# A windowed-attention and feed-forward kernel with a written-out plan: split first transposes, later masks and sink values, a new load order

## The chip, the cores and the metric

The kernel runs on one core of a Trainium2 chip. The metric is device time in microseconds (us) of one execution. Its engines are PE (matrix multiply), DVE (vector), ACT (scalar, exponentials), POOL (here it issues the loads from memory and a few small fills) and SP (here it issues stores and DMA transposes).

## The reference

```python
scores = scale * np.matmul(q, k.transpose(0, 1, 3, 2))      # (4, 8, 768, 64) inputs
keep = is_sink | in_window                                  # 4 sink keys, window of 128 back
a = softmax(np.where(keep, scores, -1e9))
attn = np.matmul(a, v)                                      # 4 batches x 8 heads
x = attn.transpose(0, 2, 1, 3).reshape(3072, 512)
out = ((x @ w1) * (x @ w2)) @ w3 @ w_out                    # (3072, 512) fp32
```

Attention over a sliding window with four sink keys feeds a two-branch product network. w1 and w2 are 512 x 1024, w3 is 1024 x 1024, w_out 1024 x 512.

## The kernel before

**The work.** The kernel folds w3 and w_out into one matrix `w3o` of 1024 x 512 at the start, so each token block needs gates (line 744: x times w1 and x times w2), a product (759) and one projection (774). Attention and network are done per batch b = 0..3, in two halves c of 384 tokens. Heads go in pairs r = 0..3. In a half, q and k are transposed (`qkT`), scores (588) go to the PSUM ring `sc`, ACT makes exponentials (606), DVE multiplies by a mask (612), PE multiplies by v and by the sink values (664, ring `av` of one bank), DVE normalises (674, 679) into `xs`, and `xs` is transposed into `xT` for the gates. Matmul results that are not scores or av go through the three banks of the ring `mm`.

**The fold.** The first KA = 3 row blocks of w3 are transposed for each of eight columns j (350), copied (`w3t`, five buffers) and accumulated for all j (358); the accumulation holds one `sc` pair and one `mm` bank from its first group to its last. Row blocks 3 to 7 follow singly (381 transposes, 388 products). Each needs `w3-i`, and the products need all of w_out (`wo-0-1` to `wo-6-8`).

**q and k.** Batch 0 loads blocks of heads (`early`) and transposes them on PE (438). Its first two head pairs come by separate fp32 loads on SP and ACT and are cast (234). Batch 1 loads blocks of 128 tokens (`near`) and transposes them on PE (461). Batches 2 and 3 load into `big`, which the fold must have left, and are transposed by DMA on SP (478), as are their `xs` (720). A name such as `q1-5` in the list of loads is tensor, batch and block.

**The order.** Every step is an `Op` with an engine (or either of ACT and DVE), a guessed duration, dependencies, a priority (a smaller number goes first) and ring buffers that it takes and frees. A planner written in the kernel simulates the engines when the program is built: at each step it takes the operation that can start with the least wait, then the one of the best priority. Its choice is the order of the instructions on each engine, and nothing is reordered on the chip. POOL is the exception: it takes its operations in the order of the list `LOADS`, at most eight loads in flight. A load's guessed landing is the running total of transfer times plus `LAND`, plus a margin `unsure`; a DMA transpose or store issued before 120 us gets a margin `LATE`. These margins change no instruction, only when the planner counts on data. Where it sees a gap on PE before 45 us it fills it with multiplications of zeros (853).

Priorities: the fold's steps have FOLD_J + j and FOLD_I + 4i; batch 0's attention 1 to 4; later attention `1000 + 200 * (b - 1) + LEAD + 200 * SPREAD * part`, where `part` goes from 0 to 1 through a batch; gates of batch b `1000 + 200 * b + 100 * c + 8 * dt`; projections from `1150 + 200 * b + 100 * c`. A load of batch 3 waits for transposes of batch 2, and for the landing of the batch 3 load DEEP places back.

The masks for batches 1 to 3 are made by `late_masks` (261, 263), the sink values of a batch by `sv` (512).

Of the kernel before, what the change touches and what calls it, by code (L numbers as in the profile page):

```python
# [21 lines left out]
def kernel(  # L22
# [22 lines left out]
    P = 128  # L45
# [3 lines left out]
    QC = NB // NC  # L49
    TOK = QC * P  # L50
# [16 lines left out]
    ident = home("ident", [P, P])  # L67
    tri = home("tri", [P, P])
    maskt = home("maskt", [P, 1, 12 * P])
    vst = home("vst", [P, B, D], FP32)  # L70
    pick = home("pick", [P, H], FP32)
# [10 lines left out]
    qN = {0: early[0], 1: near[0]}  # L82
    kN = {0: early[1], 1: near[1]}
# [24 lines left out]
    class Ring:  # L108
# [9 lines left out]
        a=a_home, ab=ab_home, o=o_home, sc=sc_home, av=av_home, mm=mm_home).items()}  # L118
# [1 line left out]
    HOP = 0.12  # L120
    LAND = 1.9
    TUS = 1.3
    LATE = 2.0
    ops = []

    class Op:
# [11 lines left out]
    PE, ACT, DVE, POOL, SP = "pe", "act", "dve", "pool", "sp"  # L138
    EITHER = (ACT, DVE)
    turn_of = [None]  # L140

    def copy(out, in_):
        (nc.scalar.copy if turn_of[0] == ACT else nc.vector.tensor_copy)(out, in_)  # L143

    def cols(n, k=1):
        return k * (n / 2400.0 + 0.0025)

    def act_us(n):
        return 0.165 + n / 1200.0

    def dve_us(n, x=1.0):
        return 0.15 + n / 960.0 / x
# [12 lines left out]
    def pool_op(us, fn, deps=()):  # L165
        return Op(POOL, us, fn, deps)

    KA, LEAD, SPREAD = 3, -30, 0.9
    FOLD_J, FOLD_I = 3.5, 1010
    DEEP = 3  # L170
    FUSED = (1, 2, 3)
    KINDS = (0, 2, 2, 2)
    QK_BY_DMA = ((2, 0), (2, 1), (3, 0), (3, 1))
    X_BY_DMA = ((2, 0), (2, 1), (3, 0), (3, 1))

# [46 lines left out]
    op_vst = []  # L222
# [8 lines left out]
    got = {}  # L231
# [5 lines left out]
    for r in range(2):  # L237
        for n, dst in enumerate((kN, qN)):
            i = 2 * r + n
            got["kq"[n], 0, 0, r] = cast((DVE, ACT)[n], 0.5, dst[0][:, 0, 2 * r:2 * r + 2, :],  # L240
                                         first_home[i][:, 0:TOK].rearrange("p (h m) -> p h m", h=2), st[i])
    LOADS = """k0-0-4 v0-0 ident q0-0-4 pick w3j-2-4 v0-1 tri v0-2 w3j-0-1 w3j-4-6 w3j-1-2 wo-0-1 w3-6
        wo-1-2 wo-2-4 w3j-6-8 wo-4-6 wo-6-8 w3-5 w3-3 w3-4 v0-5 w3-7 k1-4 q0-1-0 k0-1-0 w2 w0 w3
        v0-3 k1-0 v0-4 w1 q1-0 q1-1 k1-1 q1-2 k2-1 q1-3 v1-2 k1-2 k1-5 k2-2 v1-1 v1-0 q1-4 q2-1
        q2-2 k2-0 k1-3 v2-0 q1-5 q2-0 v1-3 q3-5 v1-4 q3-0 v3-2 k2-3 q2-3 k2-5 v3-0 v1-5 k2-4 v2-2
        q2-4 q3-2 q2-5 v3-5 k3-0 v2-1 k3-5 k3-4 q3-3 v2-5 v3-4 k3-2 k3-1 v2-4 q3-1 v3-1 v3-3 k3-3
        q3-4 v2-3"""

    def masks(part):
        m = maskt[:, 0, :].rearrange("p (k q) -> p k q", q=P)  # L250
# [27 lines left out]
    for key in LOADS.split():  # L278
        n = [int(x) for x in key[2 if key[:2] == "wo" else 3 if key[:3] == "w3j" else 1:].split("-") if x.isdigit()]
        if key == "ident":  # L280
            op_ident = pool_op(0.3, lambda: nc.gpsimd.affine_select(
                ident[:], ident[:], compare_op=ALU.is_equal, fill=0.0, base=0, pattern=[[1, P]],
                channel_multiplier=-1), [op_i1])
# [21 lines left out]
        elif key[0] in "kq":  # L305
            _, c, h0 = n
# [8 lines left out]
    op_mask_late = Op(DVE, 0.7, late_masks, [op_mask], prio=30)  # L315
    op_cols = Op(DVE, 0.35, pick_cols, [op_pick], prio=3)
# [11 lines left out]
    fold_done = []  # L328
# [15 lines left out]
    for j in range(KFF):  # L344
        x = []
# [14 lines left out]
        a = Op(PE, cols(P, KA), t3, [got["w3j", j], op_ident], FOLD_J + j, takes=["mm"])  # L360
# [14 lines left out]
    for i in range(KA, KFF):  # L375
        x, y = [], []
# [16 lines left out]
        pr = FOLD_I + 4 * i  # L393
        a = Op(PE, cols(P, KFF), t3, [got["w3", i], op_ident], pr, takes=["mm"])
# [4 lines left out]
        fold_done.append(m_)  # L399
        fold_done.append(Op(EITHER, (act_us(DM), dve_us(DM)), fmc, [m_], 0, frees=[(m0, "mm")]))  # L400

    for late in in_big:
        late.deps += fold_done
    pieces = {
# [12 lines left out]
    for b in range(B):  # L417
        kind = KINDS[b]
        T = qkT_home[b % 2]
# [3 lines left out]
        tp_of = {}  # L423
        base = 10 * b

        def when(part, early):
            return 1000 + 200 * (b - 1) + LEAD + 200 * SPREAD * part if b else early
        if b == 0:
            for c in range(NC):
                for r in range(NP):  # L430
                    x = []

                    def tps(b=b, c=c, r=r, x=x):
                        tp = transposed(x[0].slot["mm"], 6 * P).rearrange("p (s j m) -> p s j m", s=2, m=P)
                        for s, src in ((0, kN[b]), (1, qN[b])):
                            for j in range(QC):
                                for e in range(2):
                                    nc.tensor.transpose(tp[64 * e:64 * e + 64, s, j, :],  # L438
                                                        src[:, c, 2 * r + e, j * D:(j + 1) * D], ident[:])

                    def tpc(T=T, c=c, r=r, x=x):
                        tp = transposed(x[0].slot["mm"], 6 * P).rearrange("p (s j m) -> p s j m", s=2, m=P)
                        for s in range(2):
                            copy(
                                T[:, r, s, c * TOK:(c + 1) * TOK].rearrange("p (m j) -> p m j", j=QC),
                                tp[:, s, :, :].rearrange("p j m -> p m j"))
                    a = Op(PE, cols(P, 6) + 0.12, tps, [got["k", b, c, r], got["q", b, c, r], op_ident],
                           base + 1 + r * 0.1, takes=["mm"])
                    x.append(a)
                    tp_of[c, r] = Op(EITHER, (2 * act_us(3 * P), 2 * dve_us(3 * P)), tpc, [a],  # L450
                                     base + 1, frees=[(a, "mm")])
        else:
            for c in range(NC):
                for r in range(NP) if (b, c) not in QK_BY_DMA else ():
                    x = []

                    def tps(b=b, c=c, r=r, x=x):
                        tp = transposed(x[0].slot["mm"], 6 * P).rearrange("p (s j m) -> p s j m", s=2, m=P)
                        for s, src in ((0, kN[b]), (1, qN[b])):
                            for j in range(QC):  # L460
                                nc.tensor.transpose(tp[:, s, j, :],
                                                    src[:, QC * c + j, r * P:(r + 1) * P], ident[:])

                    def tpc(T=T, c=c, r=r, x=x):
                        copy(
                            T[:, r, :, c * TOK:(c + 1) * TOK],
                            transposed(x[0].slot["mm"], 6 * P).rearrange("p (s m) -> p s m", s=2))
                    a = Op(PE, cols(P, 6), tps,
                           [got[n, b, QC * c + j] for n in "kq" for j in range(QC)] + [op_ident] + war,
                           when((r / 4 + c) / 2 - 0.1 if kind != 1 else r / 4 + c / 50 - 0.1, 0), takes=["mm"])  # L470
                    x.append(a)
                    tp_of[c, r] = Op(EITHER, (act_us(6 * P), dve_us(6 * P, 2)), tpc, [a], base + 1, frees=[(a, "mm")])
        turned = {}
        if any((b, c) in QK_BY_DMA for c in range(NC)):
            for kb in range(NB):
# [21 lines left out]

        def tdep(c, r, b=b, tp_of=tp_of, turned=turned):
            return sum(([turned[s, kb] for s in range(2) for kb in range(3 * c_, 3 * c_ + 3)]
                        if (b, c_) in QK_BY_DMA else [tp_of[c_, r]] for c_ in range(c + 1)), [])  # L500

        def sk(b=b, T=T):
            for e in range(2):
# [5 lines left out]
        x = []  # L509
# [3 lines left out]
                                 vst[:, b:b + 1, :].to_broadcast([P, H, D]),  # L513
                                 pick[:, :, None].to_broadcast([P, H, D]))
        warv = list(all_av[b - 2]) if b >= 2 else []
        op_sv = Op(DVE, dve_us(512), sv, op_vst + [op_cols] + warv, when(0, base + 2))

        groups = [(2, 3), (3, 6)] if kind != 1 else [(2, 6)]
        op_es, sinks_at = {}, {}
        for q0, q1 in groups:  # L520
            x = []
# [12 lines left out]
            if b in FUSED:  # L534
                at = (1 if q0 == 2 else 5 if kind == 0 else 3)
# [3 lines left out]
            a = Op(PE, cols(w) + 0.22, ss, [op_sk] + sum([tdep(c, r) for c in cs for r in range(NP)], []) + warv,  # L539
                   when(0.5 if q0 == 3 else 0, base + 2), takes=["mm"])  # L540
# [24 lines left out]
        for n_v, visit in enumerate(visits):  # L565
            x = []
# [60 lines left out]
        for n_u, (c, r) in enumerate(order):  # L627
            x = []
# [13 lines left out]
            frees = []  # L642
# [23 lines left out]
            a = Op(PE, us, avf, list(dict.fromkeys(deps)), when(n_u / 8, base + 3 + 0.01 * n_u), takes=["av"] + (["xs"] if first else []), frees=frees)  # L666
# [21 lines left out]
        for c in range(NC):  # L688
            holder = [None]
            if (b, c) not in X_BY_DMA:  # L690
                evs = []
                for n_h in range(2):
                    x = [holder]
# [9 lines left out]
                    def xtc(n_h=n_h, x=x):  # L703
                        copy(x[0][0].slot["xT"][:, 2 * n_h:2 * n_h + 2, :],
                                              transposed(x[1].slot["mm"], 6 * P).rearrange("p (r m) -> p r m", r=2))
                    a = Op(PE, cols(P, 6), xtp, [norm[c, 2 * n_h], norm[c, 2 * n_h + 1]], when(c / 2 + (n_h + 1) / 4 if kind != 1 else n_h / 2 + 0.5, base + 2.5), takes=["mm"],
                           frees=[(xs_first[c], "xs")] if n_h else [])
                    x.append(a)
                    ev = Op(EITHER, (act_us(6 * P), dve_us(6 * P, 2)), xtc, [a] + ([holder[0]] if n_h else []), base + 2.5,
                            takes=["xT"] if n_h == 0 else [], frees=[(a, "mm")])  # L710
# [5 lines left out]
            else:  # L716
                evs = []
                for j in range(QC):
                    def xtd(c=c, j=j, holder=holder, xs_first=xs_first):
# [3 lines left out]
                            takes=["xT"] if j == 0 else [],  # L723
                            frees=[(xs_first[c], "xs")] if j == QC - 1 else [])
# [7 lines left out]
    for b in range(B):  # L732
        for c in range(NC):
# [3 lines left out]
            for dt in range(KFF):  # L737
                pr = 1000 + 200 * b + 100 * c + 8 * dt
                x = [holder]
# [10 lines left out]
                def acopy(y=y):  # L750
# [4 lines left out]
                        takes=["mm"], frees=[(holder, "xT")] if dt == KFF - 1 else [])  # L755
                y.append(g2)

                def amul(dt=dt, y=y, abh=abh):
                    nc.vector.tensor_mul(abh[0].slot["ab"][:, dt, :], y[1].slot["a"][:], y[2].slot["mm"][:, 0:TOK])  # L759
                am_ = Op(DVE, dve_us(TOK), amul, [g2, ac] + ([abh[0]] if dt else []), 0, takes=["ab"] if dt == 0 else [],  # L760
                         frees=[(g2, "mm"), (ac, "a")])
# [3 lines left out]
            for mi in range(QC):  # L765
                m = QC * c + mi
                x = []
                last, oh = b == B - 1 and m == NB - 1, []
                for n0, n1 in ([(0, 256), (256, 384), (384, 512)] if last else [(0, 512)]):
                    x = []  # L770
# [33 lines left out]
    ready = {e: [o for o in ops if e in o.us_on and not o.missing] for e in free}  # L804

    def unsure(at):
        return 0.0 if at < 40.0 else 1.0

    def wants(o, e):
        at = max([d.done + (0.0 if d.ran == e == PE else HOP) for d in o.deps], default=0.0)  # L810
# [124 lines left out]
```

## Time and profile before

| what | value |
|---|---|
| median of 8 runs | 200.91 us (200.4 to 201.48) |
| the profiled execution: time, span | 200.4 us, 198.7 us |
| busy PE, DVE, ACT, POOL | 191.1, 112.6, 100.2, 73.0 us |
| granted PE clock | 1.00 |
| gates (744), projections (774) | 512 and 208 matmuls, busy 89.9 and 45.6 us |
| DMA queue of the loads | 91.6% of 16 engines' span |

The span runs from the first to the last instruction; the profiled execution's own time has 1.7 us around it. Times in the text are from the start of the span. A row of the timeline gives start, duration, engine, line, operation, destination and sources, count and, in brackets, the idle time of the engine before it and what ended it. A row of the waits gives the waiting instruction, what released it, total wait, times and longest wait. Matmuls overlap: one of 512 columns shows 379 ns, but four in a row end 0.86 us after the first began, 0.216 each.

A load's landing is when its completion count arrives. Landings in the order of issue, for the loads that the text names: w3j-0-1 12.40, wo-0-1 15.17, w3-6 16.44, wo-1-2 17.08, wo-6-8 22.32, q0-1-0 30.97, k0-1-0 33.00, w2 35.63, w0 38.35, w1 46.27, k1-2 53.46, q1-5 68.00, v1-3 70.81.

### The profile page before, as it was taken

The page shows a single profiled execution, that of the slowest core. Times are in us where ns is not written, and L with a number is a line of the kernel's source. Part 1 is how long each engine was busy: PE and PEld are TensorE (multiplying, and loading weights), DVE is VectorE, ACT ScalarE, POOL GpSimd, SP SyncE. Part 2 cuts the span into 40 slices and gives each one's busy share as a digit, 9 for nine tenths or more (in the row PEclk, how much of TensorE's full clock was granted, in tenths as well). Part 3 has the DMA queues.
Part 4 walks back from the last instruction along what each step waited for, and adds up shares of the span by engine and source line. Part 5 has one row for each costly group of instructions (what it writes and reads, how often), then busy time and mean ns, then how long its engine had stood idle before and what let it go on. Part 6 is the DMA issues. An engine that isn't in the chain of part 4 may idle for free.

```text
span 198.7 us, 4523 instructions
## 1 busy us (share of the span) xinstructions
PE 191.1 (96%) x1815; PEld 116.8 (59%) x1815; DVE 112.6 (57%) x258; ACT 100.2 (50%) x162; POOL 73.0 (37%) x96
## 2 busy tenths in 40 slices
PE   7979999999999799999999999999999999999993
PEld 6746555556666565666566556555665566555443
DVE  3987313688579588877388633435886653324200
ACT  3785444864375387663356723348377324343232
POOL 7996673687983676925930000000000000000000
PEclk9999999999999999999999999999999999999999
DMA  6999999999999999999999235554504225020133
GB/s 173 175 174 196 204 186 195 194 176 159 154 171 159 154 157 131 169 120 154 173 201 159 35 127 148 147 105 101 116 0 105 83 79 111 0 106 0 56 124 140
DMA packets 98181, 26.42 MB, mean 133 GB/s; under 512 B 86896, under 2 KB 94576, under 8 KB 98160
## 3 DMA queue, kind: packets, MB, share of 16 engines
q0 software_dynamic: 73584, 14.29, 91.6%
q1 hardware_dynamic: 23888, 11.38, 27.1%
q10 hardware_dynamic: 688, 0.46, 0.7%
q8 instruction: 14, 0.23, 0.5%
q14 instruction: 7, 0.06, 0.1%
HBM read 29.39 MB, written 6.29 MB: 180 GB/s over the span
## 4 chain that ended last, share of the span: by engine, by line
PE 60%; DMA 24%; POOL 9%; SPq 2%; issue 2%; ACT 0%; POOLq 0%
PE mm L744 30%; PE mm L774 19%; DMA w_sb<-in_moe_w_dram 10%; DMA big<-in_moe_w_dram 8%; DMA near<-in_q_dram 6%; PE av L664 5%; PE sc L588 4%; POOL big L160 4%; POOL vN L160 3%; POOL near L160 1%; SPq L478 1%; DMA qkT<-big 1%; POOL early L160 1%; SPq L720 1%; PE mm L700 1%
## 5 line engine op out<-in xcount | busy, mean ns | idle before, releaser
L744 PE MATMUL mm<-xT,w_sb 128*128 128x384 bf16 x512 | 89.9, 326 | 0.0
L744 PEld LDWEIGHTS <-w_sb 128*128 128x128 bf16 x512 | 47.7, 98 | 32.7 <-issue 2.6
L759 DVE TENSOR_TENSOR ab<-a_sb,mm 128x384 bf16<-128x384 f32 x64 | 35.3, 552 | 32.4 <-PE mm L744 29.3
L774 PE MATMUL mm<-w3o,ab 128*128 128x512 bf16 (+2 forms) x208 | 45.6, 363 | 0.0
L606 ACT ACTIVATE ex<-sc 128x1024 bf16<-128x1024 f32 (+2 forms) x49 | 43.7, 943 | 3.7 <-PE sc L588 3.5
L143 ACT COPY a_sb<-mm 128x384 f32<-128x384 f32 x51 | 24.4, 478 | 38.5 <-PE mm L744 20.9
L612 DVE TENSOR_TENSOR am<-ex,maskt 128x1024 bf16<-128x1024 bf16 (+2 forms) x49 | 29.8, 622 | 0.1
L774 PEld LDWEIGHTS <-ab 128*128 128x128 bf16 x208 | 18.9, 98 | 17.8
L143 ACT COPY o_sb<-mm 128x512 f32<-128x512 f32 (+2 forms) x23 | 12.6, 549 | 29.4 <-PE mm L774 29.3
L160 POOL DMA_DIRECT2D vN<-in_v_dram x24 | 21.3, 887 | 8.1 <-DMA big<-in_q_dram 5.9
L664 PE MATMUL av<-vN,am 128*128 128x65 bf16 x352 | 19.0, 194 | 0.5 <-DVE xs L679 0.5
L664 PEld LDWEIGHTS <-am 128*128 128x128 bf16 x352 | 17.1, 97 | 3.9 <-issue 0.6
L679 DVE TENSOR_TENSOR xs<-av,rec 128x384 bf16<-128x384 f32 x32 | 17.7, 554 | 0.7
L674 DVE RECIPROCAL rec<-av 128x6 f32<-128x6 f32 x32 | 6.2, 193 | 16.3 <-PE av L664 16.3
L588 PE MATMUL sc<-qkT 64*128 64x128 bf16 (+1 forms) x248 | 14.7, 241 | 0.4 <-DMA qkT<-big 0.4
L160 POOL DMA_DIRECT2D big<-in_q_dram x12 | 10.5, 884 | 7.8 <-DMA big<-in_k_dram 2.6
L664 PE MATMUL av<-vsb,es 128*128 128x130 bf16 x64 | 12.9, 220 | 0.0
L588 PEld LDWEIGHTS <-qkT 64*128 64x128 bf16 x248 | 8.1, 94 | 6.2 <-issue 4.6
L160 POOL DMA_DIRECT2D big<-in_k_dram x12 | 10.6, 886 | 2.4 <-DMA big<-in_q_dram 1.0
L143 DVE COPY qkT<-mm 128x384 bf16<-128x384 bf16 (+1 forms) x14 | 7.2, 551 | 5.7 <-PE mm L438 3.1
L143 DVE COPY a_sb<-mm 128x384 f32<-128x384 f32 x13 | 7.2, 557 | 5.1 <-PE mm L744 5.1
L388 PE MATMUL mm<-big,w3t 128*128 128x512 bf16 x40 | 9.5, 379 | 0.0
(64 smaller groups left out, 138.2 us busy)
## 6 DMA issues: line engine op xcount, KB each, us to landing
out_dram<-o_sb SPq DMA_DIRECT2D x23, 256.0 KB
vN<-in_v_dram POOLq DMA_DIRECT2D x24, 128.0 KB, 9.0
w_sb<-in_moe_w_dram POOLq DMA_DIRECT2D x8, 256.0 KB, 10.7
big<-in_k_dram POOLq DMA_DIRECT2D x12, 128.0 KB, 9.8
big<-in_q_dram POOLq DMA_DIRECT2D x12, 128.0 KB, 9.8
big<-in_moe_w_dram POOLq DMA_DIRECT2D x5, 256.0 KB, 9.2
big<-in_moe_w_out_dram POOLq DMA_DIRECT2D x3, 256.0 KB, 7.5
near<-in_k_dram POOLq DMA_DIRECT2D x6, 128.0 KB, 8.2
```

Source lines behind the costliest of these rows:

```text
L143: (nc.scalar.copy if turn_of[0] == ACT else nc.vector.tensor_copy)(out, in_)
L160: op = Op(eng, us, lambda: (nc.gpsimd if eng == POOL else nc.sync).dma_start(out=out, in_=in_), deps)
L388: nc.tensor.matmul(x[2].slot["mm"][:], x[1].slot["w3t"][:, j, :], wo_sb[:, j, :], start=(j == 0), stop=(j == KFF - 1))
L588: nc.tensor.matmul(sc[:, e, c * P:(c + n) * P], T[hp, r, 0, kb * P:(kb + 1) * P], T[hp, r, 1, qb * P:(qb + n) * P], start=True, stop=True)
L606: nc.scalar.activation(y[1].slot["ex"][:, :, 0:w], y[0].slot[key][:, :, 0:w], ACTF.Exp, scale=scale)
L612: nc.vector.tensor_mul(y[2].slot["am"][:, :, 0:w], y[1].slot["ex"][:, :, 0:w], maskt[:, :, m0:m0 + w].to_broadcast([P, 2, w]))
L664: nc.tensor.matmul(o, lhs, rhs, start=(i == 0), stop=(i == len(todo) - 1), skip_group_check=True)
L674: nc.vector.reciprocal(x[1].slot["rec"][:], av_of(x[0].slot["av"])[:, :, :, D:VW])
L679: nc.vector.tensor_mul(xs_first[c].slot["xs"][:, :, r * P:(r + 1) * P].rearrange("p k (e d) -> p k e d", d=D), av_of(x[0].slot["av"])[:, : ...
L744: nc.tensor.matmul(pg[:, 0:TOK], w_sb[:, kk, dt * P:(dt + 1) * P], holder[0].slot["xT"][:, kk, :], start=(kk == 0), stop=(kk == NP - 1))
L759: nc.vector.tensor_mul(abh[0].slot["ab"][:, dt, :], y[1].slot["a"][:], y[2].slot["mm"][:, 0:TOK])
L774: nc.tensor.matmul(x[0].slot["mm"][:, 0:n1 - n0], abh[0].slot["ab"][:, kk, mi * P:(mi + 1) * P], w3o[:, kk, n0:n1], start=(kk == 0), stop= ...
```

## The change

Five things. For batch 0's first two head pairs of the first half, the transposes of k and q become two steps, so that k's need not wait for q; and for all of batch 0 the copies of k's and q's transposes are two steps that may go to different engines. The late masks, and the sink values of batches 1 to 3, wait for the fold's first accumulation (`fold_done[0]`). The planner's margins change: `LATE` from 2.0 to 1.5; `unsure` from 1.0 after 40 us to 0.5 up to 56 and 2.5 after. The priorities change: LEAD, SPREAD, FOLD_J, FOLD_I, and DEEP from 3 to 2. The list of loads has a new order from the twelfth load on.

```diff
-    LATE = 2.0
+    LATE = 1.5
...
-    KA, LEAD, SPREAD = 3, -30, 0.9
-    FOLD_J, FOLD_I = 3.5, 1010
-    DEEP = 3
+    KA, LEAD, SPREAD = 3, -10, 0.6
+    FOLD_J, FOLD_I = 0.5, 980
+    DEEP = 2
...
+    APART = ((0, 0), (0, 1))
...
-    LOADS = """k0-0-4 v0-0 ident q0-0-4 pick w3j-2-4 v0-1 tri v0-2 w3j-0-1 w3j-4-6 w3j-1-2 wo-0-1 w3-6
-        wo-1-2 wo-2-4 w3j-6-8 wo-4-6 wo-6-8 w3-5 w3-3 w3-4 v0-5 w3-7 k1-4 q0-1-0 k0-1-0 w2 w0 w3
-        v0-3 k1-0 v0-4 w1 q1-0 q1-1 k1-1 q1-2 k2-1 q1-3 v1-2 k1-2 k1-5 k2-2 v1-1 v1-0 q1-4 q2-1
-        q2-2 k2-0 k1-3 v2-0 q1-5 q2-0 v1-3 q3-5 v1-4 q3-0 v3-2 k2-3 q2-3 k2-5 v3-0 v1-5 k2-4 v2-2
-        q2-4 q3-2 q2-5 v3-5 k3-0 v2-1 k3-5 k3-4 q3-3 v2-5 v3-4 k3-2 k3-1 v2-4 q3-1 v3-1 v3-3 k3-3
-        q3-4 v2-3"""
+    LOADS = """k0-0-4 v0-0 ident q0-0-4 pick w3j-2-4 v0-1 tri v0-2 w3j-0-1 w3j-4-6 w3j-1-2 wo-1-2 wo-0-1
+        wo-2-4 wo-4-6 w3j-6-8 w3-6 wo-6-8 w3-3 w0 w3-5 q0-1-0 w3-4 w3-7 k0-1-0 w1 v0-4 v1-2 w3
+        v0-5 v1-1 v0-3 w2 q1-1 q1-0 k1-2 k1-0 k1-1 k2-0 k1-4 q1-2 q1-5 q3-0 k1-3 q2-1 q2-2 k2-1
+        v1-5 v1-0 q1-4 k2-2 q1-3 q2-5 k1-5 k3-5 q2-3 v1-4 v1-3 q2-0 v2-1 v2-4 v2-0 k2-3 q3-3 k3-0
+        k2-4 v2-2 q3-4 q2-4 k2-5 k3-2 v3-5 v3-2 q3-1 q3-2 v3-1 v3-4 v2-5 v3-3 v2-3 v3-0 k3-3 q3-5
+        k3-1 k3-4"""
...
+    op_mask_late.deps.append(fold_done[0])
...
-                    a = Op(PE, cols(P, 6) + 0.12, tps, [got["k", b, c, r], got["q", b, c, r], op_ident],
-                           base + 1 + r * 0.1, takes=["mm"])
+                    if (c, r) in APART:
+                        a = Op(PE, cols(P, 3) + 0.12, lambda f=tps: f((0,)), [got["k", b, c, r], op_ident], pr, takes=["mm"])
+                        a2 = Op(PE, cols(P, 3) + 0.12, lambda f=tps: f((1,)), [got["q", b, c, r], a], pr)
+                    else:
+                        a = a2 = Op(PE, cols(P, 6) + 0.12, lambda f=tps: f((0, 1)),
+                                    [got["k", b, c, r], got["q", b, c, r], op_ident], pr, takes=["mm"])
                     x.append(a)
-                    tp_of[c, r] = Op(EITHER, (2 * act_us(3 * P), 2 * dve_us(3 * P)), tpc, [a],
-                                     base + 1, frees=[(a, "mm")])
+                    tk = Op(EITHER, (act_us(3 * P), dve_us(3 * P)), lambda f=tpc: f(0), [a], base + 1)
+                    tq = Op(EITHER, (act_us(3 * P), dve_us(3 * P)), lambda f=tpc: f(1), [a2], base + 1, frees=[(a, "mm")])
+                    tq.after = tk
+                    tp_of[c, r] = [tk, tq]
...
-        op_sv = Op(DVE, dve_us(512), sv, op_vst + [op_cols] + warv, when(0, base + 2))
+        op_sv = Op(DVE, dve_us(512), sv, op_vst + [op_cols] + warv + ([fold_done[0]] if b else []), when(0, base + 2))
...
-        return 0.0 if at < 40.0 else 1.0
+        return 0.0 if at < 40.0 else 0.5 if at < 56.0 else 2.5
```

More of the change, by code (lines that the diff above doesn't have):

```diff
@@ L431, with tps @@
                     x = []
-                    def tps(b=b, c=c, r=r, x=x):
+                    def tps(part, b=b, c=c, r=r, x=x):
                         tp = transposed(x[0].slot["mm"], 6 * P).rearrange("p (s j m) -> p s j m", s=2, m=P)
-                        for s, src in ((0, kN[b]), (1, qN[b])):
+                        for s in part:
+                            src = (kN, qN)[s][b]
                             for j in range(QC):
@@ L439, in tps, with tpc @@
                                                         src[:, c, 2 * r + e, j * D:(j + 1) * D], ident[:])
-                    def tpc(T=T, c=c, r=r, x=x):
+                    def tpc(s, T=T, c=c, r=r, x=x):
                         tp = transposed(x[0].slot["mm"], 6 * P).rearrange("p (s j m) -> p s j m", s=2, m=P)
[L443 to L446, printed above, removed]
-                    a = Op(PE, cols(P, 6) + 0.12, tps, [got["k", b, c, r], got["q", b, c, r], op_ident],
-                           base + 1 + r * 0.1, takes=["mm"])
+                        copy(
+                            T[:, r, s, c * TOK:(c + 1) * TOK].rearrange("p (m j) -> p m j", j=QC),
+                            tp[:, s, :, :].rearrange("p j m -> p m j"))
+                    pr = base + 1 + r * 0.1
+                    if (c, r) in APART:
[4 more added lines that the diff above has]
+                                    [got["k", b, c, r], got["q", b, c, r], op_ident], pr, takes=["mm"])
                     x.append(a)
-                    tp_of[c, r] = Op(EITHER, (2 * act_us(3 * P), 2 * dve_us(3 * P)), tpc, [a],
-                                     base + 1, frees=[(a, "mm")])
+                    tk = Op(EITHER, (act_us(3 * P), dve_us(3 * P)), lambda f=tpc: f(0), [a], base + 1)
+                    tq = Op(EITHER, (act_us(3 * P), dve_us(3 * P)), lambda f=tpc: f(1), [a2], base + 1, frees=[(a, "mm")])
+                    tq.after = tk
+                    tp_of[c, r] = [tk, tq]
         else:
@@ L471 @@
                     x.append(a)
-                    tp_of[c, r] = Op(EITHER, (act_us(6 * P), dve_us(6 * P, 2)), tpc, [a], base + 1, frees=[(a, "mm")])
+                    tp_of[c, r] = [Op(EITHER, (act_us(6 * P), dve_us(6 * P, 2)), tpc, [a], base + 1, frees=[(a, "mm")])]
         turned = {}
@@ L499, in tdep @@
             return sum(([turned[s, kb] for s in range(2) for kb in range(3 * c_, 3 * c_ + 3)]
-                        if (b, c_) in QK_BY_DMA else [tp_of[c_, r]] for c_ in range(c + 1)), [])
+                        if (b, c_) in QK_BY_DMA else tp_of[c_, r] for c_ in range(c + 1)), [])
         def sk(b=b, T=T):
```

## The prediction

> **What bounds the kernel now.** I read the page first: its engine table and slices.
>
> ```profile
> PE 191.1 (96%) x1815; PEld 116.8 (59%) x1815; DVE 112.6 (57%) x258; ACT 100.2 (50%) x162; POOL 73.0 (37%) x96
> ...
> PE   7979999999999799999999999999999999999993
> ```
>
> PE sets the time. It is short of full only in slices 1, 3 (0 to 15 us), 14 (about 65 to 70 us) and at the end. The change adds and removes no matmul of the result, so it can gain only where PE idles or multiplies zeros. The waits by engine, for PE, name the idle places:
>
> ```profile
> PE mm L853 <- DVE zeros L220: 1.3, 1, 1.3
> PE mm L461 <- DMA near<-in_q_dram: 1.1, 1, 1.1
> PE mm L350 <- DMA big<-in_moe_w_dram: 0.9, 1, 0.9
> PE av L664 <- DVE xs L679: 0.5, 1, 0.5
> PE sc L588 <- DMA qkT<-big: 0.4, 1, 0.4
> ```
>
> The timeline of PE puts 1.07 at 66.97 to 68.05 us (the transposes of batch 1's second half wait for its last q block), 0.45 at 133 us (scores of batch 3 wait for a DMA transpose), 0.88 at 11.6 and 0.50 at 14.2 us. Zeros (L853) fill about 1.8 us between 5.7 and 8.3, 0.9 between 9.9 and 11.1, 0.44 at 15.1, 0.13 at 16.4 and 0.13 at 40.5. The end after the last matmul (195.5 to 198.7) is untouched.
>
> Is the idleness before 16 us recoverable? The timeline of PE and that of POOL, around 22 us:
>
> ```profile
> 21.68 0.59 PE L358 MATMUL sc<-big,w3t 128*128 128x512 bf16 x2
> 22.11 0.38 PE L358 MATMUL mm<-big,w3t 128*128 128x512 bf16 x1
> 22.36 0.59 PE L358 MATMUL sc<-big,w3t 128*128 128x512 bf16 x2
> ```
>
> ```profile
> 22.60 0.87 POOL L160 DMA_DIRECT2D early<-in_k_dram  x1 [0.78 <-DMA big<-in_moe_w_out_dram]
> ```
>
> POOL keeps eight loads in flight and issues about 0.28 us after one lands: this row shows wo-6-8 landing at 22.32. The L358 matmuls at 22.36 are the seventh of eight groups, the first that needs wo-6-8. By 22.33 PE had run everything else whose data was there: all 24 L350 transposes, 24 first-half scores, four AV groups, both x transposes, six L358 groups, and the eight transposes of w3-6. So PE is supplied just in time at 22.3, by loads, and the gaps before it are waiting for loads that the change leaves in the same set: up to wo-6-8 the new list holds the same bytes. From there to 66.5 PE loses only the 0.13 of zeros. **What can be gained at all is 0.13 + 1.07 + 0.45 = 1.65 us.**
>
> **The change part by part.** The profiled execution took 200.4 for a span of 198.7 (1.7 around it); the median of the runs is 200.91, 0.51 above it. I sum against the span and move the median by the sum.
>
> Split transposes and copies: k of the first pair waits for its own cast alone. Twelve L438 transposes at 4.97 become six at about 4.5 (k's cast ends 4.38) and six at 4.97 (q's ends at 4.74); the two L143 copies, 5.86 to 6.88 one after the other on DVE, can run on both engines: about 0.5 off the first scores. Late masks (L261, L263: 8.23 to 8.76) and batch 1's sink values (L512, 16.26 to 16.94) move behind the first L358 group, each with a wait on it. That frees 0.43 before the first mask multiply at 8.68 and 0.68 between two AV groups. What queues on DVE behind the new waits are evictions and normalisations; the readers come at 56 us (masks) and 62 us (sinks), so I cost the waits at nothing; without that cover they cost at most the 0.7 us of each step. All of these gains end before 22.3 and buy nothing: PE would wait longer for wo-6-8. **0.**
>
> Loads before 22.3: wo-0-1 changes places with wo-1-2 and w3-6 goes behind w3j-6-8. wo-1-2 then lands at 15.17 and wo-0-1 one step (0.64, what wo-1-2 took) later, at about 15.8; the fold's first accumulation, which ran at 15.53 and is the first in its chain, starts 0.3 later at least. From 15.53 to 22.33 PE had 6.8 us of work without a gap over 0.13, so every 0.1 lost there is lost for good, unless DVE's freed time brings an AV group (about 0.4) before it. FOLD_J 0.5 also places the fold ahead of AV and scores in the order, so AV groups can be queued behind its wait. Bounds: -0.05 (nothing lost, and the landing binds) to +0.9 (the AV groups queue behind a full wait). I take **+0.3**, nearest to the 15.53 row.
>
> From 22.3 to 46: w0 moves up (22.3 + 1.25 for w3-3 + 2 x 1.3: it lands near 26 instead of 38), the second-half blocks of q and k about 1 us either way. Work released from 22.3 to 36.8 is then two L358 groups 1.3, five folds of 0.45 + 1.73, w0's gates 2.6, transposes 1.65, scores 1.75, sinks 0.3: 18.5 us for 14.5, a bank of 4 where PE had 1.3 at 41.8 (8 gates of 0.163). The 0.13 of zeros goes: **-0.13**, between -0.13 and +0.3.
>
> Batch 1's blocks: landings in this stretch are 0.85 to 0.95 apart. The first half is complete with the eighth block after the weights, in both lists: 53.46 before, used at 53.98. The planner's margin for landings there is cut from 1.0 to 0.5, which is the 0.52 of slack that this row has. Cover gone, a late landing is a wait: 0 to +0.5, taken **+0.2**. The last block was 19th after the weights (q1-5, 68.0) and is 21st now (k1-5): by the old 21st landing, 70.8. PE wanted it at 66.97 with a margin of 1.0; with 2.5 the planner puts it 1.5 later for the margin and two blocks (1.8) later for the place: 70.3, against 70.8. PE has batch 0's gates (L744) and projections (L774) meanwhile, 9.5 us of which stand after 66.5 in the old order (16 L744 of 0.163 and 32 L774 of 0.216). So of 1.07 some 0 to 0.5 stays, but it is reached with q's transposes already run; **-1.07**, bounds -1.07 to +0.5 (a longer wait, if the extra DMA transposes of batch 2 fall before it).
>
> The Trainium skill (DMA: Bandwidth & Descriptors, "Anatomy of one DMA — SWDGE (gpsimd) path") fits such a transfer as about 2.0 us plus bytes over 436 GB/s. By it two blocks of 256 KB read would move the last landing by an estimated 1.2 us, not 1.8, and a load would land in some 2.6 us, where the profile has medians of 7.8 to 9.8; the rows decide.
>
> The two edits at LATE and DEEP: 0.5 us less margin for DMA transposes issued before 120 us, and later batch 3 loads wait for the landing two back. q3-4 must now wait for q3-3 with only three others between, and q2-4, k2-5 stand behind it on POOL: at most one landing time of a queue four deep short, about 1.5 us, at 92 us. Their scores ran at 101.2. Bounds 0 to +0.5, taken **+0.15**.
>
> LEAD and SPREAD: a batch's attention starts 20 units of priority later and ends 40 earlier (120 units wide, was 180). Batch 2's second half then gets off SP earlier, ahead of batch 3's transposes, which queue behind it on SP until 133: **-0.45**, bounds -0.45 to +2 (the third rival).
>
> Sum: 0 + 0.3 - 0.13 + 0.2 - 1.07 + 0.15 - 0.45 = -1.0. Span 197.7, that execution 199.4, median 199.9.
>
> One rule speaks against anything that leaves PE idle longer: the clock gate. The windows show the granted clock at 1.00 in every stretch, with idle gaps up to 1.07. The first 33 zero matmuls took 3.70 us, 112 ns each, against 54 ns for later ones.
> The Trainium skill (TensorE: Matmul & The Clock Gate, "What's actually happening") halves the clock after an idle window of about 3.4 us. By it a gap of 1.5 us ahead of 22.3 stays free, and one over 3.4 would cost an estimated 3.4/2 = 1.7 us more; nothing here shows such a gap.
>
> **The rivals.** Forecast, the waits at 68 and 133 go: 199.9, its own range 199.3 to 200.5. Chance 0.50.
>
> Nothing to see: the plan's new order only moves the waits. The last block lands 2.8 later than before, so a wait of about 1 returns near 70, and the head loses 0.3: -1.0 + 1.07 = +0.1, time 201.0. For it: the planner had 1.0 of margin and still missed by 1.07, and the list puts the block two places back. Against it: the margin grows by 1.5. Chance 0.14 (200.5 to 201.3).
>
> Slower: attention packed into two thirds of its stretch makes DVE the bound. Per batch DVE needs 11 mask multiplies x 0.68, 8 x 0.55 (L679), 8 x 0.19 (L674) and about 1.0 for sinks: 14.4 us. PE's attention work is about 7.5; beside the gates DVE has 0.552 per 1.30 us of PE, 0.425 per us. A stretch W needs 14.4 + 0.425 (W - 7.5) of DVE. Old stretches: batch 1 54 to 93, batch 2 81 to 122, batch 3 132.6 to 161.1. The windows with PE full show DVE at most like this:
>
> ```profile
> 70.00:80.00 10.00, 10.00 (x107) 5.92 (x105) 8.45 (x18) 8.04 (x11) 7.34 (x9) 1.00 2.25 143
> ```
>
> At that 0.85 the stretch must be 26 us. Two thirds of 28.5 is 19 us for batch 3: 19.3 of DVE, 22.7 us at 0.85, so 3.7 of wait; batches 1 and 2 (26 and 27 us) escape. Less the 1.5 of the waits at 68 and 133 it is +2.2: 203.1. It decides from the point where a batch's attention takes under about 23 us (a wait of 1.5, which cancels the gain). Against it: batch 3 ran in 28.5 with PE at 20.00 of 20 in the window 140 to 160. The head's +0.9 and the block's +0.5 lead to this side too. Chance 0.36 (201.3 to 203.1 and a little beyond).
>
> **How the numbers follow.** 0.2% is 0.4 us, about what runs of this kernel can tell from no change (200.4 to 201.48). Faster 0.50, same 0.14, slower 0.36, straight from the cases. Lower end: 200.91 - 1.65 and 0.3 for the spread of medians, 199.0. Upper end: 202.9, short of the full price of the third case; about one in ten lies above and less below.
>
> **What would show it.** Right: no PE wait above 0.3 on `near` about 70 us, none on `qkT` about 133, the seventh L358 group still at 22.3 to 22.7 however early the first scores run, PE's last matmul at 194.5. The step on the head is wrong if that group starts at the landing and the total of PE's waits before it did not grow as the scores came earlier, or if it starts after 22.7. The forecast is wrong if PE waits for DVE or ACT in rows over 0.5, or if batch 3's stretch is under 23 us with DVE over 0.9.

## The result and the profile after

The changed kernel takes 199.40 us (median of 11 runs, 198.82 to 199.98) against 200.98 (32 runs, 200.31 to 201.85): the ratio is 0.9921, interval 0.9904 to 0.9938, so 1.58 us less. A second session gave 0.9939 (0.9909 to 0.9968). The profiled execution took 199.28 for a span of 197.6; the profiled one of before is among the quickest of its kernel (200.4), so the two traces differ by only 1.1 us, and 0.4 to 0.5 of the gain is in no trace shown. A few executions ran over 1.5% above the quickest of their kernel; the ratios leave them out, the medians do not.

Lines of the changed kernel lie further down: 350 is 351, 358 is 359, 381 is 382, 388 is 389, 438 is 441, 461 is 470, 588 is 597, 664 is 673, 744 is 753, 774 is 783, 853 is 862. The page of the changed kernel, engine table and slices of PE:

```profile
PE 191.0 (97%) x1815; PEld 116.7 (59%) x1815; DVE 115.6 (59%) x262; ACT 98.2 (50%) x158; POOL 73.2 (37%) x96
...
PE   7899999999999999999999999999999999999993
```

The number of matmuls and PE's busy time are the same; slice 14 is full now. The waits of PE after the change:

```profile
PE mm L862 <- DVE zeros L221: 1.3, 1, 1.3
PE mm L441 <- ACT qkT L143: 0.4, 1, 0.4
PE mm L441 <- DVE early L235: 0.4, 1, 0.4
PE mm L382 <- DMA big<-in_moe_w_dram: 0.4, 1, 0.4
PE sc L597 <- ACT ex L615: 0.2, 1, 0.2
PE mm L351 <- ACT qkT L143: 0.2, 1, 0.2
```

The waits on `near` (1.1 at 68 us) and on `qkT` from a DMA transpose (0.4 at 133) are gone. New are 0.4 for a load of w3, 0.4 for the cast of the second pair's k (`early`), and 0.4 for a copy of transposes. The timeline of PE around 22 us, and where batch 1's second half now starts:

```profile
20.61 0.67 PE L862 MATMUL sc<-zeros 128*128 128x128 bf16 x9
...
22.01 0.59 PE L359 MATMUL sc<-big,w3t 128*128 128x512 bf16 x2
22.44 0.38 PE L359 MATMUL mm<-big,w3t 128*128 128x512 bf16 x1
22.65 0.59 PE L359 MATMUL sc<-big,w3t 128*128 128x512 bf16 x2
23.09 0.38 PE L359 MATMUL mm<-big,w3t 128*128 128x512 bf16 x1
23.83 0.62 PE L382 MATMUL mm<-ident,big 128*128 128x128 bf16 x8 [0.37 <-DMA big<-in_moe_w_dram]
...
70.55 1.03 PE L783 MATMUL mm<-w3o,ab 128*128 128x512 bf16 x4
71.41 0.83 PE L470 MATMUL mm<-ident,near 128*128 128x128 bf16 x12
```

wo-6-8 landed at 21.47 and w3-3, right behind it, at 23.79: the last groups of the fold's first accumulation are done and PE waits for w3-3. The last block of batch 1 (k1-5) landed at 70.49 and is asked for at 71.41, with a projection (L783) put before it.

To see where time went I sum what PE lost in each stretch: over successive matmuls, the time from start to start less the median of that form after 45 us in the kernel before; multiplications by zeros count whole. Starts are used because ends overlap: the four products at 70.55 show 1.03 us, but the next matmul starts 0.86 after the first. Score groups always carry a part of this loss, about the same in every kernel. Values in us, one profiled execution each; ratios are against before in the same session, whose median was 200.98 for the first row, 201.12 for the repeat, 201.23 for head_alone to old_loads and 200.67 for list_margin to old_sp.

| kernel | 0-24 | 24-54 | 54-120 | 120-140 | 140-end | median us | ratio (interval) |
|---|---|---|---|---|---|---|---|
| before | 10.47 | 1.48 | 4.60 | 1.24 | 1.12 | 200.98 | 1 |
| changed | 10.66 | 1.95 | 3.39 | 0.62 | 1.13 | 199.40 | 0.9921 (0.9904-0.9938) |
| changed, again | 10.56 | 1.91 | 3.36 | 0.62 | 1.13 | 199.64 | 0.9939 (0.9909-0.9968) |
| head_alone | 11.81 | 1.63 | 4.96 | 0.76 | 1.13 | 201.13 | 0.9982 (0.9950-1.0014) |
| margin_alone | 10.54 | 1.48 | 3.82 | 1.57 | 1.13 | 200.00 | 0.9937 (0.9909-0.9965) |
| old_margin | 10.80 | 1.91 | 4.57 | 0.60 | 1.14 | 201.48 | 1.0007 (0.9976-1.0038) |
| old_loads | 11.11 | 1.62 | 4.37 | 0.66 | 3.60 | 202.19 | 1.0038 (1.0012-1.0064) |
| list_margin | 11.03 | 2.26 | 4.06 | 0.61 | 1.13 | 201.02 | 1.0008 (0.9980-1.0036) |
| old_fold | 11.82 | 2.23 | 4.09 | 0.60 | 1.15 | 201.31 | 1.0029 (1.0001-1.0056) |
| old_sp | 10.84 | 1.92 | 3.59 | 1.20 | 1.14 | 200.05 | 0.9948 (0.9923-0.9973) |

Before to changed, column by column: +0.19, +0.47, -1.21, -0.62 and +0.01, together -1.16, about the difference of the spans (1.1).

### The profile page after: what moved, and what is told of

It reads as the page before. It is cut to its first block, busy times and chain, and to the rows that moved or that the text cites. A ratio compares the mean times of both kernels' runs of the same rounds, so it can differ in the third digit from the quotient of the medians.

```text
span 197.6 us, 4514 instructions
## 1 busy us (share of the span) xinstructions
PE 191.0 (97%) x1815; PEld 116.7 (59%) x1815; DVE 115.6 (59%) x262; ACT 98.2 (50%) x158; POOL 73.2 (37%) x96
## 4 chain that ended last, share of the span: by engine, by line
PE 84%; POOL 7%; DMA 5%; ACT 1%; issue 1%; DVE 1%; POOLq 0%
PE mm L753 42%; PE mm L783 21%; PE av L673 7%; PE sc L597 5%; DMA big<-in_moe_w_dram 5%; PE mm L389 5%; POOL big L160 4%; PE mm L470 1%; POOL vN L160 1%; PE mm L709 1%; ACT qkT L143 1%; POOL early L160 1%; PE mm L382 1%; PE mm L535 1%; DVE w3t L143 0%
## 5 line engine op out<-in xcount | busy, mean ns | idle before, releaser
L783 PE MATMUL mm<-w3o,ab 128*128 128x512 bf16 (+2 forms) x208 | 45.9, 363 | 0.0
L783 PEld LDWEIGHTS <-ab 128*128 128x128 bf16 x208 | 18.6, 98 | 17.7 <-issue 0.6
L143 ACT COPY o_sb<-mm 128x512 f32<-128x512 f32 (+2 forms) x21 | 11.4, 545 | 24.2 <-PE mm L783 24.1
L143 DVE COPY w3t<-mm 128x1024 bf16<-128x1024 bf16 (+1 forms) x8 | 4.5, 563 | 6.8 <-PE mm L382 6.1
## 6 DMA issues: line engine op xcount, KB each, us to landing
big<-in_k_dram POOLq DMA_DIRECT2D x12, 128.0 KB, 10.2
big<-in_q_dram POOLq DMA_DIRECT2D x12, 128.0 KB, 10.2
```

The lines of the kernel that those rows point to most:

```text
L783: nc.tensor.matmul(x[0].slot["mm"][:, 0:n1 - n0], abh[0].slot["ab"][:, kk, mi * P:(mi + 1) * P], w3o[:, kk, n0:n1], start=(kk == 0), stop= ...
```

## The experiments

**The head alone.** The kernel before with `APART`, the two copy steps and `fold_done[0]` as a dependency of the late masks and sink values.

> The kernel before with only the head of the change: split transposes and copies of batch 0, late masks and sink values held until the fold's first accumulation. Old loads, margins and priorities. My theory (the gain before 22 us is absorbed by the wait for wo-6-8): time within 0.4 us of before; PE loses some 0.5 us less before 20 us and as much more between 20 and 24, with the seventh L359 group at 22.3 to 22.5. The rival (the head is on the path): 0.5 to 0.7 us faster, with that group at 21.8. The waits near 68 and 133 us stay, about 1.1 and 0.45, unless the new order happens to move them.

By the ratio 0.36 us under before, with an interval that reaches from 1.0 less to 0.3 more: neither nothing nor the rival's 0.5 to 0.7 is ruled out. The timeline of PE of head_alone shows what binds; in that execution wo-6-8 landed at 23.65:

```profile
21.96 0.59 PE L359 MATMUL sc<-big,w3t 128*128 128x512 bf16 x2
22.40 0.38 PE L359 MATMUL mm<-big,w3t 128*128 128x512 bf16 x1
23.69 0.59 PE L359 MATMUL sc<-big,w3t 128*128 128x512 bf16 x2 [0.92 <-DMA big<-in_moe_w_out_dram]
```

Six groups are done and the seventh starts with the landing. But the trace doesn't show a gain being absorbed: its first scores ran at 6.72 instead of 7.00, and by 20 us PE had lost no less than in before (10.4 against 10.2 by the same sum), so the 0.5 that I expected ahead of 20 us was not there to absorb. The test of the wait itself is the next run.

**Three loads ahead of wo-6-8.**

```diff
-        wo-1-2 wo-2-4 w3j-6-8 wo-4-6 wo-6-8 w3-5 w3-3 w3-4 v0-5 w3-7 ...
-        v0-3 k1-0 v0-4 w1 ...
+        wo-1-2 wo-2-4 w3j-6-8 wo-4-6 v0-3 v0-4 v0-5 wo-6-8 w3-5 w3-3 w3-4 w3-7 ...
+        k1-0 w1 ...
```

> The kernel before with one thing changed: three loads of v (v0-3, v0-4, v0-5, 0.87 us each by the trace) moved ahead of wo-6-8 in the list, so that wo-6-8 and what follows up to their old places land 2.6 us later. My theory (PE has done all that is released by 22.3 us and goes on when wo-6-8 lands): PE's loss up to that landing grows by 2.0 to 2.6 and the time by as much, 202.7 to 203.6 on a chip where before is 201. The rival (PE's idle time before 22 us is a matter of the order, and work elsewhere can fill it): under 0.7 us slower.

202.55 us against 201.12, ratio 1.0071 (1.0046 to 1.0096): 0.9 to 1.9 us slower. The rival's 0.7 is out, and the size is under the 2.0 to 2.6 that I expected. The spans of the two traces do differ by that much, 201.0 against 198.7, as the trace of before is one of its quickest. In the trace wo-6-8 landed at 24.70, 2.38 later than before:

```profile
21.81 0.38 PE L358 MATMUL mm<-big,w3t 128*128 128x512 bf16 x1
22.02 2.23 PE L853 MATMUL mm<-zeros 128*128 128x128 bf16 x37
24.74 0.59 PE L358 MATMUL sc<-big,w3t 128*128 128x512 bf16 x2 [0.48 <-DMA big<-in_moe_w_out_dram]
```

Multiplications by zeros and a wait fill the whole of it. In the four kernels with the old list and fold the loss up to that group is the landing less a constant: 22.32 and 10.47 (before), 22.27 and 10.54 (margin_alone), 23.65 and 11.81 (head_alone), 24.70 and 12.86 (here, counted to 24.74): 11.7 to 11.9 us of work each time. So in these the landing sets PE's position at 24 us, and it differs between executions of one list by over 1 us. That the old kernel's quickest runs are those with an early landing is likely but not shown.

**The margins alone, and everything but the margins.** `unsure` new in the kernel before; `unsure` old in the changed one.

> The kernel before with only the new landing margins (0.5 us from 40 to 56 us, 2.5 after). My theory (the gain of the change is the wait at 68 us): PE's wait on the last q block at 68 falls from 1.07 to under 0.3 and the time by 0.8 to 1.2 us. The rival (the wait only moves): a wait of the same size appears later on and the time is within 0.4 us of before.

> The change with the landing margins of before (1.0 us after 40 us), all else as changed. My theory: the last block of batch 1 lands about 2.5 us later than before and the margin is 1.5 smaller, so PE waits 1 to 2.5 us on it near 70 us and the time is 0.8 to 2 us above the changed kernel, so at least that of before. The rival (the new list of loads or the rest gives the gain): no wait over 0.4 there and the time within 0.4 of the changed kernel.

The margins alone bring 1.23 us (0.9937); the change without them brings nothing (1.0007). The waits of PE of margin_alone name no load any more after 24 us, only the other wait, on a DMA transpose near 133, which has grown:

```profile
PE sc L588 <- DMA qkT<-big: 0.8, 1, 0.8
```

and the timeline of old_margin shows the wait back, on k1-5, landed at 70.52:

```profile
69.68 0.28 PE L470 MATMUL mm<-ident,near 128*128 128x128 bf16 x2
70.57 1.07 PE L470 MATMUL mm<-ident,near 128*128 128x128 bf16 x16 [0.61 <-DMA near<-in_k_dram]
```

It is 0.6 here, below the 1 to 2.5 that I expected, while the time is 1.8 above the change's 0.9921 of that session's 201.23; one trace does not show the size of it in a usual run. With the old list q1-5 landed at 68.0 in before, 68.5 in margin_alone and 69.8 in head_alone and in old_loads, and head_alone waited 1.4 for it. So the wait in a usual run of the old kernel may be longer than the 1.07 of its trace; that is not shown.

**The old list in the changed kernel, and the new list with the margins alone.**

> The change with the load list of before, all else as changed. My theory: the margin of 2.5 alone removes the wait at 68, so the time is within 0.5 us of the changed kernel, and by my sum, which put a loss of 0.3 on the new list, rather below it. The rival (the list carries the gain): 0.8 us or more above the changed kernel, with a wait on a load after 24 us.

> The kernel before with the new list of loads and the new margins alone: no split, no held steps, old fold priorities, LATE and DEEP. My theory (head structure and priorities are worth nothing, the margin needs the list that it goes with): within 0.5 us of the changed kernel, so some 1.2 to 1.6 below before. The rival (the fold's priority has to fit the new list, since w0 and w3-3 come before w3-5): a loss of 0.5 or more between 15 and 36 us, and the time above that of the margin alone.

Both came out against me. With the old list the change is 0.8 us slower than before. The wait near 70 is still 0.7, although the new margins are in, and two new ones stand in batch 3, by the waits of PE of old_loads:

```profile
PE mm L470 <- DMA near<-in_q_dram: 0.7, 1, 0.7
PE mm L753 <- DMA xT<-xs: 0.9, 1, 0.9
PE av L673 <- DVE xs L688: 0.9, 1, 0.9
```

And the new list on the old fold priorities loses what the margins bring: 1.0008. It loses 0.6 more than before up to 24 us and 0.8 more from there to 54, about where the rival had said. A wait near 70 is left as well, for k1-5, landed at 70.16; by the waits of PE of list_margin:

```profile
PE mm L461 <- DMA near<-in_k_dram: 0.5, 1, 0.5
```

So the new margins make the wait on batch 1's last block smaller (0.5 to 0.7 in these two, none above 0.2 in margin_alone and the change), but do not remove it in every order.

**The old fold priorities in the changed kernel.**

> The change with FOLD_J 3.5 and FOLD_I 1010. My theory: before 22.3 the loads bind whatever goes first, so PE's loss up to 24 us is within 0.3 of the changed kernel's 10.7 and the time within 0.4. The rival: with the fold behind the AV groups PE falls short of work done by 22 and the time is 0.5 us or more above.

My theory fell by the time: 201.31 us, 1.0029, where I had allowed 0.4 over the change. The trace has 11.82 lost up to 24 us, 1.2 more than the change, although wo-6-8 landed at 21.91. Part of that is the rival's: the order does leave PE short. By the timelines the planner filled gaps with 29 multiplications by zeros between 14 and 30 us, 14 more than in the change (32 in list_margin), or 0.8 us at 56 ns. But the loss up to 24 us can't be put down to it, as this execution was also slow at the start. The two kernels have the same matmuls in the same order for about the first 10 us, and here they ran at half the rate for longer. The same 17 multiplications by zeros, in the timelines of PE of the changed kernel and of old_fold, and the scores behind them:

```profile
7.04 1.12 PE L862 MATMUL mm<-zeros 128*128 128x128 bf16 x17
8.39 0.34 PE L597 MATMUL sc<-qkT 64*128 64x256 bf16 x4 [0.23 <-ACT ex L615]
```

```profile
7.60 1.99 PE L862 MATMUL mm<-zeros 128*128 128x128 bf16 x17
9.52 0.50 PE L597 MATMUL sc<-qkT 64*128 64x256 bf16 x4
```

PE is 1.1 us behind there, about as much as its extra loss up to 24 us. So the times (1.0029 against 0.9921 and 0.9939) show that with the new list the old fold priorities cost time, and list_margin fits that. The added zeros are a likely cause of part of it; how much of the 1.9 us over the change they make is not shown.

**LATE and DEEP old in the changed kernel; margins, LATE and DEEP new in the old one.**

> The change with LATE 2.0 and DEEP 3 as before. LEAD and SPREAD change no instruction's place, so the wait at 133 us that went away must have gone by these two or by the list. If by these two: the wait on qkT near 133 is back at 0.4 to 1.0 and the time up by as much. If by the list and what follows from it: no such wait, time within 0.3 us of the changed kernel. My sum had 0.15 as the price of these two edits, so 0.15 below the changed kernel by it.

> The kernel before with three numbers changed: the new margins, LATE 1.5 and DEEP 2; old list, old fold, no split and nothing held. My theory: margins take the wait at 68 us, LATE and DEEP take the one at 133 (1.02 with the margins alone), so 0.3 to 1.0 us below the margins alone and level with the whole change, 1.4 to 1.9 below before. The rival (where the wait at 133 falls is chance of the order): 0.8 to 1.4 below before, with a wait of 0.4 or more on a transpose left.

With both old, the wait on `qkT` near 135 us is back (0.3 by the waits of PE of old_sp, 0.55 at 135.44 by the loss), and the profiled span is 198.5 against 197.6 and 197.4:

```profile
PE sc L597 <- DMA qkT<-big: 0.3, 1, 0.3
```

The time, 0.9948, is not told apart from the change's 0.9921 and 0.9939. With both new in the old kernel, beside the margins, the wait at 133 went too, but the kernel took 201.93, 1.0042 (1.0025 to 1.0059): waits of 1.1 on `xT` at 147 and 0.9 on `xs` at 168, the pair that old_loads has. So the two values are not good or bad by themselves; with the old list they come with two waits in the last batch, with the new one they don't. Nor are they the only way to lose the wait at 133: list_margin, with both old, has none there (0.61 lost from 120 to 140), and head_alone nearly none (0.76).

**One copy step for k and q.**

```diff
+                    else:
+                        tk = tq = Op(EITHER, (2 * act_us(3 * P), 2 * dve_us(3 * P)), lambda f=tpc: (f(0), f(1)), [a], base + 1, frees=[(a, "mm")])
```

> The change, but the two copies of a pair's k and q stay one step on one engine, as before, except in the first two pairs of the first half. In the changed kernel q's copy on the other engine starts only when k's has ended, and PE loses 0.61 us at 36.5 in front of the fourth pair's transposes of batch 0's second half. My theory: that loss is the price of splitting the copies; here it falls under 0.2, and the time is 0.3 to 0.6 us below the changed kernel. The rival (the three banks of the ring mm bind there whichever engine copies): the loss stays above 0.4 and the time within 0.3 of the changed kernel.

> The change with k's and q's copies as one step outside the first two pairs, once more, because the profile of the first run was taken at a lower clock. Theory as before (the split costs 0.61 at 36.5): 0.3 to 0.6 below the changed kernel run beside it, no loss over 0.2 in front of the fourth pair. Rival: within 0.3 of it.

0.9942 and 0.9939, the same as the changed kernel (0.9939 beside the second): no gain. The gap stays, now filled with zeros, as the timeline of PE of one_copy_again shows:

```profile
35.23 1.27 PE L441 MATMUL mm<-ident,early 128*64 128x128 bf16 x36
36.43 0.51 PE L865 MATMUL sc<-zeros 128*128 128x128 bf16 x6
36.87 0.53 PE L441 MATMUL mm<-ident,early 128*64 128x128 bf16 x12
```

0.44 us between the third pair and the fourth, where the split kernel had 0.42 idle. This is what the rival said: three groups of transposes in a row fill the three `mm` banks, and the fourth has to wait for a copy, whether the copies of a pair are split or not. The old order put fold products (L388) between them.

**The changed kernel again.**

> The changed kernel itself, beside the three others: 1.2 to 1.9 below before. If the landing of wo-6-8 sets the loss up to 24 us, that loss moves from the first profile's 10.7 by as much as the landing moves from 21.5, with w3-3 right behind it.

The loss did not move with wo-6-8 (21.47, then 21.63): it went from 10.66 to 10.56, as w3-3's landing did, from 23.79 to 23.69. That is 13.13 us of work each time, and the same for old_sp (23.97 and 10.84). In these three w3-3, behind wo-6-8, is the load that binds. In old_margin, with the same list, it landed at 23.34 and PE came to it only at 23.98.

No version tried beats the changed kernel.

## Why the prediction was right or wrong, point by point

**What can be gained (1.65).** Not contradicted: the traces differ by 1.1, the medians by 1.58.

**Head, 0.** Supported by late_wo, where a late landing cost its length; head_alone alone can't tell 0 from 0.5. Inside the step, two things were wrong. The first scores came 0.34 earlier (6.66 against 7.00), not 0.5. And I had k's and q's copies run at the same time on two engines; in the changed kernel q's copy starts when k's has ended. Its timelines of DVE and ACT:

```profile
35.40 1.49 DVE L143 COPY qkT<-mm 128x384 bf16<-128x384 bf16 x3 [1.56 <-PE mm L441]
...
35.99 1.79 ACT L143 COPY qkT<-mm 128x384 bf16<-128x384 bf16 x4 [0.47 <-DVE qkT L143]
```

The first DVE copy ends at 35.95. The program has a wait there between the engines, so the split brings order, not overlap.

**Loads before 22.3, +0.3.** Measured +0.19, for another reason, so its nearness is luck. wo-0-1 landed at 15.22, not 15.8, and the first accumulation ran at 15.32, earlier than before. wo-6-8 landed at 21.47, not 22.3, and the seventh group ran at 22.01, outside the 22.3 to 22.7 that I had named as a sign of being right, and half a microsecond after the landing. The loss is in the zeros at 20.61 and, from 23.46 to 23.83, in the wait for w3-3.

**22.3 to 46, -0.13.** Wrong sign: +0.47 from 24 to 54. The bank of work was there, but PE takes its instructions in order, and the order has four groups of transposes in a row (0.61 at 36.5) and a product ahead of its copy (0.40 at 39.0). I had counted work released, not the order it is asked in.

**Batch 1's blocks, +0.2 and -1.07.** The mechanism is right: margin_alone has the gain, old_margin loses it, and the wait on the last block went and came with the margins. The landing was 70.49 against the 70.8 worked out. The smaller margin up to 56 us cost nothing in the trace: 53.86 landed, 54.65 used. The stretch 54 to 120 gave -1.21.

**LATE and DEEP, +0.15.** Wrong sign in the traces: with them old in the changed kernel the wait near 135 returns, 0.6 more loss in that stretch. The times (0.9948 against 0.9921 and 0.9939) don't tell the two apart.

**LEAD and SPREAD, -0.45, and the third rival.** The wait at 133 did go (-0.62), but not by these. With -30 and 0.9 put back into the changed kernel, or -10 and 0.6 into the old one, the built programs have the same instructions in the same order on all five engines; 0.3 for SPREAD too. The edit does nothing, so the packing that carried 0.36 of my chance could not occur. Batch 3's scores ran from 133.6 to 153.2, 132.6 to 154.4 before. I read the numbers as if they moved the attention against the gates. Even with LEAD at -500 and SPREAD at 0.9 the changed kernel comes out as the same program: with all these values the attention already goes first wherever it can start.

**The rival of a moved wait.** It did not happen in the changed kernel. It did in old_margin (0.6), and with the new margins in list_margin (0.5) and old_loads (0.7).

So the sum of -1.0 came out near the traces' -1.1 by luck as well: the largest term, -1.07, had the right cause, but four others (the loads before 22.3, 22 to 46, LATE and DEEP, LEAD and SPREAD) were wrong in sign or cause, and their errors cancelled in part. The median, 199.40, is inside the range and 0.5 below the forecast of 199.9. Of the signs named ahead, no wait above 0.3 on `near` about 70 us nor on `qkT` about 133 is left, and the last matmul ended at 194.3 where 194.5 was named. Open stays whether LATE or DEEP clears the wait at 133 in the changed kernel (they were tried together), how much of the cost of the old fold priorities with the new list is in the added zeros, and where in a usual run of before the 0.4 to 0.5 us lie that its trace does not have.

## What to carry to other kernels

Before counting a gain in a loading stage, find the first instruction that starts with a landing and ask whether all released work was done by then: if it was, a quicker step ahead of it is worth nothing and a later landing costs its full length. In an order fixed ahead of time, a margin on the landings that come latest can be worth more than any step made shorter. Parameters of a list and of priorities have to be judged together, since each alone can undo the others' gain. Compare the built orders before giving a price to a priority. And before an early loss in one trace is put down to the order, see whether the same instructions took the same time.

## What the runs showed of the hardware that I had not expected

**Short idleness was followed by half of PE's clock.** In the first profile of one_copy, w3j-4-6 landed at 15.11 instead of about 13.4. The windows of that profile (columns: PE, PEld, DVE, ACT, POOL busy, granted clock, DMA share, GB/s):

```profile
12.00:14.00 2.00, 1.53 (x25) 0.94 (x23) 1.67 (x5) 1.63 (x5) 1.91 (x3) 1.00 1.32 166
14.00:16.00 2.00, 0.84 (x12) 0.62 (x13) 1.49 (x4) 0.52 (x1) 0.60 (x1) 1.00 1.17 185
16.00:17.00 1.00, 0.80 (x19) 0.71 (x18) 0.20 (x1) 0.75 (x2) 1.00 (x3) 1.00 1.23 189
17.00:18.00 1.00, 1.00 (x8) 0.54 (x6) 0.74 (x2) 0.60 (x2) 1.00 (x2) 0.54 1.29 182
18.00:20.00 2.00, 2.00 (x7) 0.81 (x6) 1.26 (x7) 0.48 (x1) 0.92 (x3) 0.50 1.16 195
```

One wait of 1.55 us, with PE busy 2.37 of 4 us around it, was followed by 0.50 of the clock for some 3 us, and products of 512 columns were 0.43 apart instead of 0.216. The profile of margin_sp has the like: a wait of 2.2 us that ended at 14.2, then this window:

```profile
15.00:20.00 5.00, 4.78 (x45) 3.54 (x44) 3.46 (x9) 3.12 (x7) 4.07 (x7) 0.50 1.23 183
```

In the other traces the longest gap once PE runs is the 1.4 us of head_alone near 69, and the clock stays at 1.00 behind it; two cases don't make a threshold. The Trainium skill (TensorE: Matmul & The Clock Gate, "What's actually happening") has the halving after an idle window of about 3.4 us; here less than that was enough, and the measurement decides. My price for a late landing before 22 us, its own length, is too low when it also costs the clock, and the gap of 1.5 us that I called free ahead of 22.3 need not be.

**The time at which PE reaches full rate differs between executions, and the granted clock does not show it.** Multiplications by zeros start 107 ns apart at first and 56 ns apart later. This slow start is last seen between 4.2 and 5.9 us in the other traces and at 9.2 in that of old_fold, where it cost 1.1 us by the rows shown above. The page of old_fold has no row for the clock. In before, where the first 33 such multiplications took 3.70 us, the window over them gives a granted clock of 1.00 all the same, so it is the spacing of equal matmuls that tells:

```profile
0.00:10.00 10.00, 8.67 (x124) 7.39 (x125) 6.64 (x35) 5.54 (x10) 8.66 (x18) 1.00 1.27 174
```
